# PV matmuls in two halves, the last output piece on other engines, and WoB's second half in five loads instead of eight

## The chip, the cores and the metric

One core of one Trainium2 chip. The metric is the device time of one execution in microseconds; the kernel before takes 473.68 us (median of 3, 473.41 to 474.09). The parts of the change discussed here are worth tenths of a microsecond, less than the scatter of single executions. So most of the argument rests on profiles: from one profile to another the length of a stage after the start-up repeats to 0.03 us or better, unless PE (TensorE) loses time in a single *hole* (treated below), and that is fine enough to see each part.

## The reference

Two attention blocks on the same 2048 x 1024 input, 32 heads of 32, mixed by a gate.

```python
def _A_ref(x, wqkv, wo):            # linear attention
    ...
    kv = jnp.einsum("bhsd,bhse->bhde", pk, v); z = ...
    o = num / den
    return ... @ wo
def _B_ref(x, wqkv, wo):            # sliding window: 8 keys, 2 apart
    kg = k[:, :, idx_c, :]; vg = v[:, :, idx_c, :]
    attn = softmax(where(mask, einsum("bhsd,bhswd->bhsw", q, kg) * scale, -1e9))
    o = jnp.einsum("bhsw,bhswd->bhsd", attn, vg)
    return ... @ wo
g = sigmoid((x * gate_w).sum(-1, keepdims=True))
return g * a + (1 - g) * b
```

## The kernel before

The part that matters is the attention stage of block B. For each of eight chunks of four heads, 64 projection *steps* make q and k; each step is four matmuls of 64x64 weights on 512 columns. In the profile of this kernel the four of the stage's first step start 3 to 4 ns apart and are recorded as 0.40 us each, while the next steps come 0.216 us apart. Between steps, *events* are slipped in by step number: score batches (`scores`, up to 16 matmuls) and PV batches (`pv`, 32 small matmuls of 33 columns, or 16 for the last batch of a chunk).

```python
def pv(g):
    c, m0, n = BATCHES[g]
    pt, base, ns = PT[g % 2], BLOCKS[m0][0], n // 2
    o2 = po[:, :, 0:ns * 132].rearrange("p a (s i e) -> p a s i e", s=ns, i=4)
    for s_ in range(ns):
        for i in range(4):
            for dm in range(2):
                for par in range(2):
                    ...
                    nc.tensor.matmul(o2[64 * h:64 * h + w, par, s_, i, :], lhsT=pt[r, i, o:o + w],
                                     rhs=V[r, m, 4 * c + i, :], start=True, stop=True)
    ...   # VectorE: reciprocals and scaling out of po, then stores
# when (64 steps a chunk):
for g, (c, m, n) in enumerate(BATCHES):
    p_ = 64 * c + ((43, 55, 75, 86, 97) if c < KT - 1 else (43, 55, 75, 83, 92))[m // 4]
    events.append((p_, lambda g=g: scores(g)))
    events.append((p_ + (14 if c < KT - 1 or m < 8 else 12), lambda g=g: pv(g)))
```

WoB's second half is loaded near the stage's end by `load_wo(1, 0, 8)`: eight loads of 128x512 from SyncE. In the output stage each piece is scaled and stored by ScalarE and its queue; the last piece is 128x128.

```python
nc.scalar.activation(out=osb[:, 0:n], in_=st["ps"][:, 0:n], func=ACT.Copy, scale=omg[:, tb:tb + 1])
nc.scalar.dma_start(out=rows(out2, tb * P, (tb + 1) * P)[:, c0:c0 + n], in_=osb[:, 0:n])
```

The softmax here doesn't subtract the row's maximum and nothing guards it: scores larger than these inputs give would overflow.

## Time and profile before

| | before |
|---|---|
| time, median | 473.68 us |
| span of the profiled execution | 472.29 us |
| PE busy, share of the chain | 99%, 98% |
| attention stage (first q/k matmul to first output matmul) | 141.17 us |
| tail (end of the last matmul to end of span) | 2.96 us |

The page of the kernel before: the busy line, and the first line of the chain that ended last (its shares by engine).

```profile
PE 466.0 (99%) x5734; PEld 244.7 (52%) x5765; DVE 277.4 (59%) x601; ACT 169.1 (36%) x273; POOL 15.4 (3%) x30
PE 98%; DMA 1%; issue 0%; ACT 0%
```

PE never rests long enough to matter, so a change pays only where PE's own stream loses time, or after it has ended.

The timeline of PE and of its weight loads (PEld) around one PV batch; columns are start, duration (from the first start to the last end), engine, line, operation, tiles, shapes and count.

```profile
248.53 0.81 PE L388 MATMUL q_ps<-xT,WkB 64*64 64x512 bf16 x10
249.15 0.42 PE L467 MATMUL po<-V,PT 64*56 64x33 bf16 x32
249.38 0.85 PE L388 MATMUL q_ps<-xT,WkB 64*64 64x512 bf16 x12
...
248.94 0.53 PEld L467 LDWEIGHTS <-PT 64*56 64x56 bf16 x32
249.38 0.38 PEld L388 LDWEIGHTS <-WkB 64*64 64x64 bf16 x12
```

The first weight load of the PV batch starts at 248.94, 0.21 us before its matmul at 249.15: the load runs one projection step (0.216 us) ahead. After the batch the first projection weights are loaded at 249.38, just when their matmul starts: the lead is gone. The batch's 0.23 us (249.15 to 249.38) is what 32 matmuls take when four start every 28.5 ns, as the first ones do in the single records, and the loss shows in the next step, which in the single records starts 237 ns later instead of 216.

The ends of the attention stage, in the same view.

```profile
217.40 0.84 PE L388 MATMUL q_ps<-xT,WkB 64*64 64x512 bf16 x12
...
358.57 1.90 PE L585 MATMUL d_ps<-WoA,pqT 128*128 128x512 bf16 x7
```

The end of the program: the timeline from the last matmuls.

```profile
468.83 0.50 PE L585 MATMUL e_ps<-WoB,OBT 128*128 128x128 bf16 x6
469.37 0.37 ACT L590 ACTIVATE osb<-e_ps,omg 128x128 bf16<-128x128 f32 x1 [0.47 <-PE e_ps L585]
469.76 0.34 ACTq L592 DMA_DIRECT2D out_dram<-osb  x1
```

SyncE's waits and drains at the last line of the program (a wait is for a semaphore; the first of the last five here ends 0.022 us after the last store has landed), from the view of that line (operation, count, minimum/median/maximum in ns, first and last start).

```profile
L639 SPq EVENT_SEMAPHORE  x7: 17/28/16728, 454.5 to 472.2; - x7
L639 SPq DRAIN  x3: 7/7/7, 471.5 to 471.8; - x3
```

PE ends at 469.33, ScalarE scales, its queue issues at 469.76. SyncE's first final wait lasts 16.7 us; the first drain comes at 471.5.

SyncE's DMA issues around the end of the attention stage.

```profile
347.34 6.52 SPq L517 DMA_DIRECT2D WoB<-in_B_wo_dram  x10
353.97 5.36 SPq L490 DMA_DIRECT2D obd<-Ob  x10
361.57 1.20 SPq L495 DMA_TRANSPOSE OBT<-obd  x1
```

### The profile page before, as it was taken

The page shows a single profiled execution, that of the slowest core. Times are in us where ns is not written, and L with a number is a line of the kernel's source. Part 1 is how long each engine was busy: PE and PEld are TensorE (multiplying, and loading weights), DVE is VectorE, ACT ScalarE, POOL GpSimd, SP SyncE. Part 2 cuts the span into 40 slices and gives each one's busy share as a digit, 9 for nine tenths or more (in the row PEclk, how much of TensorE's full clock was granted, in tenths as well). Part 3 has the DMA queues.
Part 4 walks back from the last instruction along what each step waited for, and adds up shares of the span by engine and source line. Part 5 has one row for each costly group of instructions (what it writes and reads, how often), then busy time and mean ns, then how long its engine had stood idle before and what let it go on. Part 6 is the DMA issues. An engine that isn't in the chain of part 4 may idle for free.

```text
span 472.3 us, 13144 instructions
## 1 busy us (share of the span) xinstructions
PE 466.0 (99%) x5734; PEld 244.7 (52%) x5765; DVE 277.4 (59%) x601; ACT 169.1 (36%) x273; POOL 15.4 (3%) x30
## 2 busy tenths in 40 slices
PE   8999999999999999999999999999999999999997
PEld 5444444445444444445666666666664444444444
DVE  0496689990329999999567676767560049800000
ACT  1343321102443333333555555555551134221122
POOL 3300000500000000000000000000000000000000
PEclk9999999999999999999999999999999999999999
DMA  8999970000634233527326526452563933211001
GB/s 212 212 242 374 348 239 0 0 1 0 203 123 125 95 141 129 156 96 247 107 54 108 105 53 95 100 95 51 92 158 79 196 97 78 71 53 46 34 33 46
DMA packets 98780, 55.40 MB, mean 117 GB/s; under 512 B 70178, under 2 KB 90658, under 8 KB 98722
## 3 DMA queue, kind: packets, MB, share of 16 engines
q1 hardware_dynamic: 93282, 49.84, 41.1%
q10 hardware_dynamic: 5440, 4.72, 3.0%
q8 instruction: 45, 0.74, 0.7%
q14 instruction: 13, 0.11, 0.1%
HBM read 26.10 MB, written 15.86 MB: 89 GB/s over the span
## 4 chain that ended last, share of the span: by engine, by line
PE 98%; DMA 1%; issue 0%; ACT 0%
PE q_ps L388 27%; PE d_ps L585 12%; PE pk_ps L169 12%; PE p_ps L295 12%; PE g_ps L220 12%; PE e_ps L585 11%; PE p_ps L331 9%; PE po L467 2%; PE s2b L445 2%; DMA xT<-in_A_x_dram 1%; PE kv_ps L240 0%; PE w_ps L283 0%; ACT osb L590 0%
## 5 line engine op out<-in xcount | busy, mean ns | idle before, releaser
L388 PE MATMUL q_ps<-xT,WqB 64*64 64x512 bf16 x1024 | 68.3, 377 | 0.0
L388 PE MATMUL q_ps<-xT,WkB 64*64 64x512 bf16 x1024 | 67.9, 377 | 0.0
L156 DVE TENSOR_SCALAR e<-e 128x512 f32<-128x512 f32 x64 | 27.0, 423 | 64.3 <-ACT e L155 64.3
L295 PE MATMUL p_ps<-WvB,xT 128*128 128x512 bf16 x250 | 57.3, 379 | 0.5 <-issue 0.3
L169 PE MATMUL pk_ps<-WkA,xT 128*128 128x512 bf16 x251 | 55.6, 381 | 0.9 <-DMA xT<-in_A_x_dram 0.6
L220 PE MATMUL g_ps<-pk,xrow 128*128 128x512 bf16 x251 | 55.2, 379 | 0.3
L450 ACT ACTIVATE PT<-s2b 128x928 bf16<-128x928 f32 (+4 forms) x40 | 34.2, 854 | 45.5 <-PE s2b L445 45.5
L452 DVE TENSOR_TENSOR PT<-PT,mask 128x928 bf16<-128x928 bf16 (+4 forms) x40 | 23.6, 590 | 38.2 <-ACT PT L450 38.2
L331 PE MATMUL p_ps<-WqA,xT 128*128 128x512 bf16 x187 | 43.1, 379 | 0.3
L585 PEld LDWEIGHTS <-pqT 128*128 128x128 bf16 x272 | 26.0, 98 | 29.8 <-issue 0.4
L585 PEld LDWEIGHTS <-OBT 128*128 128x128 bf16 x272 | 26.0, 98 | 29.3
L169 PEld LDWEIGHTS <-xT 128*128 128x128 bf16 x256 | 25.1, 98 | 31.2 <-DMA xT<-in_A_x_dram 0.9
L220 PEld LDWEIGHTS <-xrow 128*128 128x128 bf16 x256 | 25.0, 98 | 30.2
L295 PEld LDWEIGHTS <-xT 128*128 128x128 bf16 x256 | 24.6, 98 | 30.0 <-issue 0.9
L388 PEld LDWEIGHTS <-WkB 64*64 64x64 bf16 x1024 | 31.7, 107 | 15.4 <-issue 0.4
L388 PEld LDWEIGHTS <-WqB 64*64 64x64 bf16 x1024 | 31.4, 106 | 15.4 <-issue 0.7
L155 ACT ACTIVATE e<-pk_ps 128x512 f32<-128x512 f32 x32 | 18.9, 597 | 40.8 <-PE pk_ps L169 36.6
L300 ACT CAST tmp<-p_ps 128x512 bf16<-128x512 f32 x32 | 18.8, 590 | 37.9 <-PE p_ps L295 29.2
L585 PE MATMUL d_ps<-WoA,pqT 128*128 128x512 bf16 (+1 forms) x133 | 30.7, 369 | 0.2
L585 PE MATMUL d_ps<-WoB,OBT 128*128 128x512 bf16 (+1 forms) x134 | 30.7, 369 | 0.1
L331 PEld LDWEIGHTS <-xT 128*128 128x128 bf16 x192 | 18.8, 98 | 22.7
L585 PE MATMUL e_ps<-WoB,OBT 128*128 128x512 bf16 (+2 forms) x133 | 29.7, 363 | 0.2
(62 smaller groups left out, 484.6 us busy)
## 6 DMA issues: line engine op xcount, KB each, us to landing
vd<-tmp SPq DMA_DIRECT2D x16, 264.0 KB
xrow<-in_A_x_dram SPq DMA_DIRECT2D x4, 1024.0 KB
out_dram<-osb ACTq DMA_DIRECT2D x31, 128.0 KB
pqd<-tmp SPq DMA_DIRECT2D x12, 256.0 KB
WvA<-in_A_wqkv_dram SPq DMA_DIRECT2D x2, 1024.0 KB
WoA<-in_A_wo_dram SPq DMA_DIRECT2D x2, 1024.0 KB
WvB<-in_B_wqkv_dram SPq DMA_DIRECT2D x2, 1024.0 KB
WqA<-in_A_wqkv_dram SPq DMA_DIRECT2D x2, 1024.0 KB
```

The costliest lines, as they stand in the source:

```text
L155: nc.scalar.activation(out=e[:], in_=pj[:], func=ACT.Exp)
L156: nc.vector.tensor_scalar(out=e[:], in0=e[:], scalar1=1.0, scalar2=1e-6, op0=ALU.min, op1=ALU.add)
L169: nc.tensor.matmul(pj[:], lhsT=xT[:, kt, t * P:(t + 1) * P], rhs=WkA[half][:, kt, :], start=(kt == 0), stop=(kt == KT - 1))
L220: nc.tensor.matmul(pj[:], lhsT=xrow[:, t, kt * P:(kt + 1) * P], rhs=pk[:, t, half * 512:(half + 1) * 512], start=(t == 0), stop=(t == NB - 1))
L295: nc.tensor.matmul(st["pj"][:], lhsT=xT[:, kt, t * P:(t + 1) * P], rhs=WvB[half][:, kt, :], start=(kt == 0), stop=(kt == KT - 1))
L300: nc.scalar.copy(out=v[:, half * 16:(half + 1) * 16, 0:Dh], in_=st["pj"][:].rearrange("p (h e) -> p h e", h=16))
L331: nc.tensor.matmul(st["pj"][:], lhsT=xT[:, kt, t * P:(t + 1) * P], rhs=WqA[half][:, kt, :], start=(kt == 0), stop=(kt == KT - 1))
L388: nc.tensor.matmul(banks[o][64 * j:64 * j + 64, :], lhsT=lhsT(r, kt, j), rhs=rhs(r, kt), start=first and kt == 0, stop=kt == KT - 1, skip_ ...
L445: nc.tensor.matmul(s2b[64 * par:64 * par + 64, pair, :, o:o + w], lhsT=kts[c][r, par, k0:k0 + 64], rhs=qz[r, :, par, q0 % 512:q0 % 512 + w ...
L450: nc.scalar.activation(out=pt[:, :, 0:W_], in_=s2b[:].rearrange("p a b s -> p (a b) s")[:, :, 0:W_], func=ACT.Exp, scale=SCALE)
L452: nc.vector.tensor_tensor(out=pt[:, :, 0:W_], in0=pt[:, :, 0:W_], in1=mask[:, None, base:base + W_].broadcast_to([P, 4, W_]), op=ALU.mult)
L585: nc.tensor.matmul(st["ps"][:, 0:n], lhsT=lhsT, rhs=W[c0 // 512][:, c, c0 % 512:c0 % 512 + n], start=(side == 0 and c == 0), stop=(side == ...
```

## The change

The intent: split each PV batch so that the weight loads can get ahead again between its halves (before, their lead of 0.21 us is gone when the batch ends); use engines that are idle at the end for the last piece; free SyncE earlier.

```diff
-            def pv(g):
+            def pv(g, only):
-                for s_ in range(ns):
+                for s_ in only:
...
+                if only[-1] < ns - 1:
+                    return
...
-                events.append((p_ + (14 if c < KT - 1 or m < 8 else 12), lambda g=g: pv(g)))
+                at = p_ + (14 if c < KT - 1 or m < 8 else 12)
+                apart = 2 if c < KT - 1 or m < 8 else 0
+                for k in range(n // 2):
+                    events.append((at + apart * k, lambda g=g, k=k: pv(g, (k,))))
...
-            load_wo(1, 0, 8)
+            load_wo(1, 0, 4)
+            nc.sync.dma_start(out=WoB[1][:, 4:KT, :],
+                              in_=B_wo[4 * P:, 512:1024].rearrange("(k p) n -> p k n", p=P))
...
+                    if i == len(parts) - 1:
+                        nc.vector.tensor_scalar(out=osb[:, 0:n], in0=st["ps"][:, 0:n], scalar1=omg[:, tb:tb + 1],
+                                                scalar2=None, op0=ALU.mult)
+                        nc.sync.dma_start(out=dst, in_=osb[:, 0:n])
+                        return
```

More of the change, by code (lines that the diff above doesn't have):

```diff
@@ L589, in mm @@
                     osb = work3.tile([P, 512], BF16, name="osb", tag="e")
+                    dst = rows(out2, tb * P, (tb + 1) * P)[:, c0:c0 + n]
+                    if i == len(parts) - 1:
[3 more added lines that the diff above has]
+                        return
                     nc.scalar.activation(out=osb[:, 0:n], in_=st["ps"][:, 0:n], func=ACT.Copy,
                                          scale=omg[:, tb:tb + 1])
-                    nc.scalar.dma_start(out=rows(out2, tb * P, (tb + 1) * P)[:, c0:c0 + n], in_=osb[:, 0:n])
+                    nc.scalar.dma_start(out=dst, in_=osb[:, 0:n])
                 def side(k):
```

## The prediction

> **What bounds it now.** TensorE. The page's busy table has PE at 99% of the 472.3 us span, the chain of waits is 98% PE, the granted clock is 1.0, and the view of waits gives PE almost no idle time. Other engines have slack. Only bubbles in TensorE's own stream and the tail after it can pay.
>
> **PV batches.** In the attention stage (217.4 to 358.6 us) the timeline of single PE instructions shows a four-matmul projection step every 216 ns, score batches without loss, and a loss at each PV batch of 32 matmuls. Four PV matmuls start every 28.5 ns, so 32 should take 228 ns. From the batch's start to the next projection it takes 230 to 240, and the next step is 13 to 24 too long: 254 in the mean (31 batches). Near matmul 29 the weight load no longer runs ahead of its matmul[...]. Eight batches of 16 cost 118 to 120, plus 4 in the next step: 123. A 32-batch two steps after a score batch costs no more (252) than one after twelve (254)[...]. Two halves: 246 against 254, 8.5 ns saved. Three last batches are not split apart, so 30 are: **0.26 us**, all on the PE chain.
>
> The second half ends two steps (0.43 us) later, but nothing new should wait: reciprocals and scaling mostly stood behind the mask multiply on VectorE anyway, and the slack before the next PV, which reuses the same PSUM tile, is some 0.5 us.
>
> **Last output piece.** Before: the last matmul ends at 469.34, ScalarE scales from 469.37 to 469.73, its queue issues at 469.76, the data land at 471.23. VectorE's 128x128 read of PSUM takes 0.285 us in this trace (a broadcast multiply) against ScalarE's 0.368, so scaling saves 0.08 us[...]. But SyncE's final waits are a list: the last store's semaphore stands in the first of five, and after it four more took 62 ns each before the drain at 471.54. In the changed kernel as built the last store has the fifth wait's semaphore, so 0.25 us of waits are over beforehand. Net: **0.15 us**, between -0.1 and +0.3.
>
> **WoB.** Three load issues fewer, some 0.46 us each on SyncE (timeline, 349 to 354). The last attention stores and transposes issue 1 to 1.4 us earlier (first transpose: 361.6). PE waits for none of them: **0 us**.
>
> **Prediction.** 473.68 - 0.26 - 0.15 = 473.25 us; range 472.7 to 473.9, since medians scatter by 0.3. Faster by over 2%: 0.5%; within 2%: 99%; slower by over 2%: 0.5%.
>
> **Right or wrong.** The timeline should show PV batches of 16, two steps apart, each about 119 ns with the next step within 5 ns of 216; the attention stage 0.2 to 0.3 us shorter; no PE wait on VectorE; the first transpose at 360 to 361; the last scaling 0.3 us on VectorE, and the last SyncE wait followed at once by the drain.
>
> **What would make it wrong.** [...] a half with its own start-up cost; the next PV, or projections, waiting for delayed VectorE work; a SyncE store issuing or landing slower than ScalarE's.

In the PV part 254 and 123 ns a batch are read from the trace, and 30 x 8.5 ns make the 0.26 us. In the part on the last piece the step shows 0.08 and 0.25 us, and its net of 0.15 us stands as the estimate. The sum is: 473.68 - 0.26 - 0.15 = 473.25 us.

## The result

473.20 us (median of 6, 472.93 to 473.48) against 473.67 (median of 6) for the kernel before. The ratio is 0.9989, 95% interval 0.9977 to 1.0002. A ratio here is the mean time of one kernel's fast runs over that of the other's of the same rounds, so it is not quite the ratio of the medians quoted. The profiled executions are all at granted clock 1.0.

The page of the changed kernel, first line of the chain:

```profile
PE 98%; DMA 1%; DVE 0%; issue 0%; DVEq 0%
```

The timeline at the place of the batch shown above (PE, then its weight loads):

```profile
248.35 0.63 PE L388 MATMUL q_ps<-xT,WkB 64*64 64x512 bf16 x8
248.78 0.29 PE L467 MATMUL po<-V,PT 64*56 64x33 bf16 x15
248.90 0.38 PE L388 MATMUL q_ps<-xT,WkB 64*64 64x512 bf16 x1
248.90 0.18 PE L467 MATMUL po<-V,PT 64*56 64x33 bf16 x1
248.92 0.61 PE L388 MATMUL q_ps<-xT,WkB 64*64 64x512 bf16 x7
249.33 0.29 PE L467 MATMUL po<-V,PT 64*56 64x33 bf16 x15
...
248.87 0.11 PEld L388 LDWEIGHTS <-WkB 64*64 64x64 bf16 x1
```

Two batches of 16 (15 and one, because the last PV matmul and the first projection matmul start almost together), two steps apart. The projection weights are now loaded at 248.87, 0.03 us before their matmul: a small lead is left.

The ends of the stage:

```profile
217.09 1.27 PE L388 MATMUL q_ps<-xT,WkB 64*64 64x512 bf16 x20
...
358.12 1.90 PE L592 MATMUL d_ps<-WoA,pqT 128*128 128x512 bf16 x8
```

The stage takes 141.03 us, 0.14 less than before: about half of the predicted 0.26. The end of the program:

```profile
468.38 0.50 PE L592 MATMUL e_ps<-WoB,OBT 128*128 128x128 bf16 x6
468.98 0.35 DVE L599 TENSOR_SCALAR osb<-e_ps,omg 128x128 bf16<-128x128 f32 x1 [57.58 <-PE e_ps L592]
469.36 0.36 SPq L601 DMA_DIRECT2D out_dram<-osb  x1
```

and SyncE's waits and drains at the last line:

```profile
L652 SPq EVENT_SEMAPHORE  x7: 17/28/28, 469.8 to 471.6; - x7
L652 SPq DRAIN  x3: 7/7/7, 470.9 to 471.2; - x3
```

PE ends at 468.88 and the span at 471.66: the tail is 2.78 us, 0.18 less. From PE's end to the issue it takes 0.476 us, not 0.435: VectorE starts 0.097 us after PE's end, ScalarE had started 0.038 after it. What is shorter comes after the landing. The single records of SyncE's last five waits (end times, us) show how:

```
before: last store landed 471.227; waits end 471.249  471.314  471.376  471.439  471.501; drain 471.538
after:  last store landed 470.833; waits end 469.800  469.864  469.926  469.990  470.877; drain 470.914
```

Before, the first wait held the last store's semaphore, and four more waits of some 62 ns each followed the landing. After, four are over when the store lands.

SyncE's issues:

```profile
350.94 5.93 SPq L492 DMA_DIRECT2D obd<-Ob  x10
359.54 1.19 SPq L497 DMA_TRANSPOSE OBT<-obd  x1
```

Counted from the stage's start, the first transpose issues 1.7 us earlier (142.45 us in, not 144.17). No PE wait changed with it: the output stage, from its first matmul's start to the last one's end, takes 110.76 us in both.

What is left of the difference between the two profiles lies before the change's reach: the stretch up to the first q/k matmul is 0.30 us shorter. That is start-up scatter, treated below. So the stage seemed to owe some 0.1 us, and who had earned the tail was open.

### The profile page after: what moved, and what is told of

Same layout as the page of the kernel before. It is cut to its first block, busy times and chain, and to the rows that moved or that the text cites. A ratio compares the mean times of both kernels' runs of the same rounds, so it can differ in the third digit from the quotient of the medians.

```text
span 471.7 us, 13176 instructions
## 1 busy us (share of the span) xinstructions
PE 467.6 (99%) x5765; PEld 251.1 (53%) x5765; DVE 278.4 (59%) x602; ACT 168.7 (36%) x272; POOL 15.3 (3%) x30
## 4 chain that ended last, share of the span: by engine, by line
PE 98%; DMA 1%; DVE 0%; issue 0%; DVEq 0%
PE q_ps L388 27%; PE d_ps L592 12%; PE p_ps L295 12%; PE pk_ps L169 12%; PE g_ps L220 12%; PE e_ps L592 12%; PE p_ps L331 9%; PE po L467 2%; PE s2b L445 2%; DMA xT<-in_A_x_dram 1%; PE kv_ps L240 0%; PE w_ps L283 0%; DVE osb L599 0%; DVEq L599 0%
## 5 line engine op out<-in xcount | busy, mean ns | idle before, releaser
L388 PE MATMUL q_ps<-xT,WqB 64*64 64x512 bf16 x1024 | 69.7, 377 | 0.0
L388 PE MATMUL q_ps<-xT,WkB 64*64 64x512 bf16 x1024 | 69.0, 376 | 0.0
L388 PEld LDWEIGHTS <-WkB 64*64 64x64 bf16 x1024 | 34.0, 107 | 11.6 <-issue 0.4
L388 PEld LDWEIGHTS <-WqB 64*64 64x64 bf16 x1024 | 32.5, 107 | 11.1 <-issue 1.0
```

The source lines that it names most:

```text
L388: nc.tensor.matmul(banks[o][64 * j:64 * j + 64, :], lhsT=lhsT(r, kt, j), rhs=rhs(r, kt), start=first and kt == 0, stop=kt == KT - 1, skip_ ...
```

## The experiments

Ten runs followed: nine other kernels, and the changed one again. All were correct. The stage and the tail are read from single records of each profile: the first q/k matmul's start to the first output matmul's start, and the last matmul's modelled end to the span's end.

| run | stage us | tail us | median us (runs) |
|---|---|---|---|
| before | 141.17 | 2.96 | 473.67 (6) |
| the change | 141.03 | 2.78 | 473.20 (6) |
| e1_halves | 140.85 | 2.96 | 473.16 (6) |
| e2_tail | 141.20 | 3.02 | 473.79 (6) |
| e3_wob | 141.19 | 2.72 | 473.72 (6) |
| e4_halves_wob | 140.82 | 2.73 | 473.31 (6) |
| e5_wob6 | 141.38 | 2.84 | one run |
| e6_apart1 | 140.82 | 2.73 | one run |
| e7_quarters | 141.47 | 2.73 | 473.36 (6) |
| e8_pv_at_scores | 141.71 | 2.96 | one run |
| after_again | 140.82 | 2.78 | 473.15 (5) |
| e9_warm42 | 141.06 | 2.73 | 473.23 (5) |

The kernel before had 473.88, 473.80 and 473.65 in the three sets of rounds (e1 to e4; e5 to e8; the last two). Where there was one run, its state is unknown, and only its stage and tail are used.

### One part at a time

**e1_halves**: the PV part alone.

```diff
-            load_wo(1, 0, 4)
-            nc.sync.dma_start(out=WoB[1][:, 4:KT, :], ...)
+            load_wo(1, 0, 8)
...   # and the last piece again on ScalarE
```

> PV in halves alone; loads and tail as before. Theory[...]: about 12.5 ns saved in each of 30 split batches, so the attention stage falls from 141.17 to about 140.79 us, unless the single 0.2 us hole seen once in the changed kernel's stage comes with the halves, then 141.03; the tail from the last matmul's end to the span's end stays 2.96 us; time -0.3 us or so against before. Rival (the halves give nothing, the gain was all in the tail): stage 141.1 to 141.2.

Measured: stage 140.85, tail 2.96; ratio 0.9982 (0.9965 to 0.9999). The halves give 0.33 us of stage and nothing in the tail. The first rival, that the halves give nothing, is out. There was no such hole this time, so the halves do not need to bring one.

**e2_tail**: the last piece alone.

```diff
-                apart = 2 if c < KT - 1 or m < 8 else 0
+                apart = 0
...   # and load_wo(1, 0, 8)
```

> Last piece scaled on VectorE and stored from SyncE alone; eight loads as before. Rival to the prediction's account of the tail: the engine change itself costs about 0.04 us and gives nothing, because in this build the last store's semaphore is again in the first of the five final waits: tail 2.96 to 3.05 us. The prediction's account (the new store brings the gain of 0.15 to 0.2 us): tail 2.75 to 2.8 us. Stage 141.17.

Measured: tail 3.02 us, 0.06 *longer* than before; ratio 1.0001 (0.9981 to 1.0022). In its build the last store's semaphore is back in the first of the five waits. Its records give 0.311 us from the landing to the drain, the same as in the kernel before, and 0.476 us from PE's end to the issue, as in the full change. The first of its final waits is again a long one, 1.09 us, in the view of its last line:

```profile
L650 SPq EVENT_SEMAPHORE  x7: 17/28/1092, 469.9 to 472.0; - x7
```

**e3_wob**: five loads alone.

```diff
-            load_wo(1, 0, 8)
+            load_wo(1, 0, 4)
+            nc.sync.dma_start(out=WoB[1][:, 4:KT, :], ...)
```

> Five loads for the second half of WoB alone. The prediction gave this part 0. New theory: three fewer DMA issues move the last store from the semaphore in the first final wait to the one in the fifth, so four waits of 62 ns are over before it lands: tail 2.96 - 0.23 = 2.72 to 2.75 us, shorter than in the full change (2.78). Prediction as put: tail 2.96. Stage 141.17.

Measured: tail 2.72 us, 0.24 shorter, with the last piece still on ScalarE; ratio 0.9997 (0.9977 to 1.0017). No final wait is long now:

```profile
L646 SPq EVENT_SEMAPHORE  x7: 17/28/28, 467.5 to 473.8; - x7
```

So the part to which the prediction gave nothing earned the whole tail gain, and the part to which it gave 0.15 us cost 0.06. The builds show the link: here DMA issues take eight semaphores in rotation (in the trace of the kernel before the last eight stores, landing from 454.50 to 471.23 us, use each of the eight once, the last one number 2, counted from 0), and three issues fewer move the last store from number 2, which SyncE waits for first, to number 7, which it waits for last. The full change has it on number 7 in its trace. (This run's time, 475.65 us in the profiled execution, is a slow start; see below.)

**e4_halves_wob**: the change without the moved piece.

```diff
-                    if i == len(parts) - 1:
-                        nc.vector.tensor_scalar(...); nc.sync.dma_start(out=dst, in_=osb[:, 0:n]); return
```

> The change without its move of the last piece. If the tail gain belongs to the loads: tail 2.72 to 2.75 us and stage 140.8 (141.03 with the hole), so a span 0.04 us shorter than the full change's, which no timing will resolve; time 0.3 to 0.6 us under before. If the gain belongs to the move: tail 2.96.

Measured: stage 140.82, tail 2.73; ratio 0.9998 (0.9975 to 1.0020), with two of its six runs at 475.14 and 475.20 (see the slow start below). The tail is 0.05 us shorter than in the full change, as e2 and e3 say. No timing here resolves so little.

### Is it the place in the list of waits?

**e5_wob6**: six loads, everything else as before.

```diff
-            load_wo(1, 0, 8)
+            load_wo(1, 0, 5)
+            nc.sync.dma_start(out=WoB[1][:, 5:KT, :],
+                              in_=B_wo[5 * P:, 512:1024].rearrange("(k p) n -> p k n", p=P))
```

> The kernel before with six loads instead of eight for WoB's second half. In this build the last store's semaphore stands in the third of the five final waits. Theory (the tail gain is the place in the list of waits, 62 ns each): tail 2.96 - 2 x 0.062 = 2.83 us, halfway between eight loads (2.96) and five (2.72). Rival (fewer or larger loads shorten the tail in some other way, such as less queued work): 2.7 to 2.75 us, near that of five loads.

Measured: tail 2.84 us. Eight loads put the last store's semaphore in the first wait, six in the third, five in the fifth; the tails are 2.96, 2.84 and 2.72, and from the landing to the drain it takes 0.311, 0.186 and 0.080 us. The place in the list settles it; fewer loads as such do not. (The stage of this run, 141.38, contains a hole, though its PV is not split.)

### What the halves win, and where it ends

**e6_apart1**: e4 with the halves one step apart.

```diff
-                apart = 2 if c < KT - 1 or m < 8 else 0
+                apart = 1 if c < KT - 1 or m < 8 else 0
```

> Halves and five loads, the halves one step apart instead of two. If the lead of the weight loads is back after one step[...], the stage is 140.8 us as with two steps. If one step of 0.216 us is too short[...], the second halves cost more and the stage is 140.95 to 141.1.

Measured: stage 140.82. One step, 0.216 us, already gives the next half what two steps give it (140.82 in e4 too).

**e7_quarters**: e4 with PV in pieces of eight, one step apart.

```diff
-                for k in range(n // 2):
-                    events.append((at + apart * k, lambda g=g, k=k: pv(g, (k,))))
+                for k in range(n):
+                    events.append((at + (k if apart else 0),
+                                   lambda g=g, k=k: pv(g, (k // 2,), (2 * (k % 2), 2 * (k % 2) + 1))))
...   # and pv(g, only, quads) loops over quads in place of all four heads
```

> Halves and five loads, but PV in pieces of eight matmuls, one step apart. If the loss is the lead that a long run of short matmuls eats up, a quarter costs about its 57 ns and the stage falls by up to a further 12 ns in each of 30 batches, to 140.5 to 140.7 us. Rival (each piece has a start-up cost of its own, some 4 ns or more): stage 140.8 to 141.0. Time 0.6 us or so under before if the first holds.

Measured: stage 141.47, with one large hole after the last full PV batch, in the PE timeline:

```profile
350.68 0.83 PE L388 MATMUL q_ps<-WqA,xT 64*64 64x512 bf16 x10
351.68 0.41 PE L388 MATMUL q_ps<-WqA,xT 64*64 64x512 bf16 x4 [0.17 <-issue]
```

To leave holes out, compare the start of the last score batch, counted from the stage's start: 132.804 us before, 132.452 in e4, 132.533 in e7. The quarters lose 81 ns against the halves, 2.7 ns in each of 30 batches, two cuts more each. So the rival holds: a piece has a cost of its own, and halves are the better cut. The ratio, 0.9990 (0.9960 to 1.0021), does not tell them apart.

A sum that fits all three, an estimate from these numbers (its 6 and 22 ns are chosen so that it fits, so it tests nothing): four PV matmuls start every 28.5 ns, so 32 need 228; a batch of 32 cost 254 in all. Thirty pairs of halves saved 352 ns, so a pair costs about 254 - 352/30 = 242; four quarters cost 2.7 more, 245. Take 4 ns per piece (the excess in the step after the lone batches of 16 before): quarters 228 + 16 = 244, halves 228 + 8 plus 6 for the lead that two halves still lose, a whole batch 228 + 4 plus 22 for the lead that it loses.

**e8_pv_at_scores**: the kernel before, with the first PV batch of each chunk straight behind a score batch.

```diff
-                events.append((p_ + (14 if c < KT - 1 or m < 8 else 12), lambda g=g: pv(g)))
+            for g, (c, m, n) in enumerate(BATCHES):   # after all the score events
+                p_ = ...
+                events.append((p_ + (12 if m == 0 else 14 if c < KT - 1 or m < 8 else 12), lambda g=g: pv(g)))
```

> The kernel before with the first PV batch of each chunk moved straight behind a score batch, no projection step between them. [...] such a PV loses 15 to 40 ns more than at its old place: from the score batch to the next one 5035 to 5060 ns against 5019. Short-lead account ([...]score matmuls start every 12.7 ns and leave the lead whole): no more loss, 5015 to 5025 ns.

The PE timeline of e8 where the score batch now leads into the PV batch, and the next score batch:

```profile
247.63 0.38 PE L445 MATMUL s2b<-qz,kt 64*64 64x112 bf16 x16
247.83 0.42 PE L467 MATMUL po<-V,PT 64*64 64x33 bf16 x32
...
252.66 0.39 PE L445 MATMUL s2b<-qz,kt 64*64 64x112 bf16 x16
```

and the same two score batches in the kernel before:

```profile
245.68 0.38 PE L445 MATMUL s2b<-qz,kt 64*64 64x112 bf16 x16
...
250.70 0.39 PE L445 MATMUL s2b<-qz,kt 64*64 64x112 bf16 x16
```

Measured in single records: 5034 to 5036 ns in six of the eight chunks, where the kernel before has 5019 to 5020 (the first chunk has 5047 against 5031; the third, 5060, has a small hole). So 14 to 17 ns more are lost: at the lower edge of the expectation's first band, 5035 to 5060, or just under it, and outside the 5015 to 5025 of the short-lead account. What is measured is that the same PV batch costs more straight behind a score batch. The author's reading, that the two share one lead, was not shown: a cost of going from one kind of small matmul straight to another was not tested apart. In the records of the second chunk, the weight loads' lead of 27 ns first shortens about 160 ns into the PV batch here (to 24 and 20 ns), and about 200 ns into it before. Once the lead is gone, weight loads follow each other every 8 ns in these records; counting the matmul of each, that is one instruction every 4 ns.

### The hole

**after_again**: the changed kernel unaltered.

> The changed kernel once more. If the 0.2 us hole in its attention stage (between the sixteenth and seventeenth score batch) is an accident of one execution, such as a late fetch of PE's instructions, it is gone or elsewhere: stage 140.80 to 140.85 us without a hole. If it belongs to the change, it is at the same place and the stage is again 141.03. Tail 2.78 us either way. Median 473.2 to 473.4.

Measured: stage 140.82, tail 2.78; 473.15 us (5 runs), ratio 0.9989 (0.9976 to 1.0001). The chain of waits around the place of the hole, in the first profile of the changed kernel:

```profile
274.22 0.20 PE s2b L445 x14
274.43 0.91 PE q_ps L388 x15
275.33 0.27 PE po L467 x12
```

and in this one:

```profile
274.01 0.20 PE s2b L445 x14
274.21 0.84 PE q_ps L388 x12
275.06 0.10 PE po L467 x9
```

The hole is gone: in single records it is 2.915 us from this score batch to the next one, as in the kernel before, against 3.105 in the first profile. The whole stage gain of the change is therefore 0.35 us, and the first profile showed 0.14 only because PE lost 0.19 us there and some 0.04 in the next stretch.

Five of the twelve profiles have a hole of 0.18 to 0.57 us in the stage (the change, e5, e7, e8, e9), also without split PV. Their places are not random. In e5, e7 and e8 the hole begins between the same two of the stage's matmuls, numbers 3897 and 3898 counted from 0, in the middle of a step. In e9, whose warm-up has five matmuls more, it comes five earlier. In the change's first profile it comes 2304 earlier, which is 18 times 128. A matmul and its weight load are two instructions in the trace, so the places lie whole blocks of 256 instructions apart. The profile has two DMA queues of the kind "instruction". The larger moved 45 packets of 16 KiB, 0.74 MB in all; the change's profile records 11,537 PE instructions (5765 matmuls, 5765 weight loads, 7 others), about 256 for each packet.

The packets' landings fit as well. Count the PE instructions started (twice the weight loads) when a packet lands, less 256 for each packet before it. In the profile of the kernel before this stays between 162 and 340 for all 45 packets, and that is why this queue is taken to carry PE's instructions; nothing in the profile names its engine. For packet 38 (from 0) this is 362, 362, 356 and 354 in e7, e8, e9 and e5, which have holes of 0.57, 0.37, 0.24 and 0.18 us; 346 in e1, which lost 0.03 us there, and in e6, which lost nothing; and 342 or less in the other six. For packet 20, 18 earlier, it is 386 in the change's first profile and 378 or less in all others. So in these twelve profiles the holes go with packets that land late by this count, from 354 on at the one place and at 386 at the other. No run delayed a packet on purpose, so that the late landing causes the hole was not shown, and why some land late stays open.

### The slow start, and a candidate

Single runs took 475 us or more, up to 476.5: of the kernel before 2 of 11, 3 of 11 and 0 of 9 in the three sets, one or two of six in e2, e3, e4 and e7, the only one of e8, none of 11 of the change. They count as fast runs and widen the intervals above. The profiled executions of e3 and e8 were among them. The chain of waits at the first projection matmuls, in e3 and then in the kernel before:

```profile
5.72 4.83 PE pk_ps L169 x12
```

```profile
5.56 3.16 PE pk_ps L169 x12
```

In e3 the first ten of these matmuls start 402 to 427 ns apart and then 216; in the kernel before two do; in seven of the twelve profiles none does. The wide spacing is about half the pace; what sets it was not shown, and the clause of the e9 expectation that named a cause is cut. The last warm-up matmul starts at 4.63 us in e3, and PE then waits for data, idle 0.78 us. But this idle time alone does not decide: it was 0.83 us in e1 and e4 and 0.91 in e2, which have no slow start. The spacing changes where the trace's record of the granted clock begins: at 9.95 us in e3, 10.11 in e8, 6.41 in the kernel before, and 3.7 to 5.2 us, before the projections, in the seven profiles without a slow start. What sets that moment was not tested. The profile's printed granted clock reads 1.0 all the while, in e3 too (4 to 10 us): the trace has no clock record before 9.95 us there, and the view counts time without one as full clock.

**e9_warm42**: e4 with a longer warm-up.

```diff
-            warm_up(37)
+            warm_up(42)
```

> Halves and five loads, with 42 warm-up matmuls instead of 37, a candidate to beat both. Some executions lose up to 2 us because the first ten projection matmuls start 427 ns apart instead of 216; the first ones come after PE sat idle for 0.5 to 0.8 us. [...] filling it leaves 0 to 3 slow starts and no run above 475 us, median 472.9 to 473.3. If not, single runs of 475 or more remain.

Measured: 473.23 us (5 runs, none above 473.62), ratio 0.9991 (0.9977 to 1.0004); no slow start in its profile. But the kernel before had none either in its nine runs of this set, so this proves nothing about the warm-up, and e9 is not shown to beat the change.

## Why the prediction was right, and where it was not

The time was right: 473.25 predicted, 473.20 measured, 473.15 in the repeat. It tests little: the stated range, 472.7 to 473.9, also holds the kernel before (473.67), so a change worth nothing would have passed too. That the center came so close is partly luck, since one part was too small and another was credited to the wrong edit. The steps under it were right in part.

- *What bounds it.* Right: PE is 98% of the chain in both. Outside the attention stage and the tail, the stages from the second matmul group to the output matmuls take the same time to 2 ns in all profiles.
- *PV batches, 0.26 us.* What was measured held: behind a split batch the projection weights are again loaded 0.03 us before their matmul, two steps are enough (one is, too: stage 140.82 us in both), and nothing on VectorE made PE wait. Why the lead is lost and comes back was not shown. The size was too small: 0.35 us (e4 and the repeat), 11.8 ns a batch instead of 8.5. The mis-sized term is the half's cost, 121 ns in place of 123. In the first profile a hole hid 0.21 us of the gain.
- *"Last output piece ... net: 0.15 us".* The sum came near the tail's 0.18 us, but the step failed: it credited the moved piece with a semaphore's place in the list of waits that this piece did not change. The move alone lengthened the tail by 0.06 us (e2): VectorE's 0.351 us saved almost nothing against ScalarE's 0.368, where 0.285 had been taken from another operation, and from PE's end to the issue it is 0.04 us longer.
- *"WoB ... 0 us".* Wrong, and the other side of the same error: it is right that PE waits for none of these loads, but three issues fewer shift the rotation of DMA semaphores, and that is worth 0.24 us at the end (e3, with e5 halfway as the wait list says). The first transpose came 1.7 us earlier, not 1 to 1.4, and gained nothing, as predicted.

Stage 0.35 and tail 0.18 make 0.53 us; the medians differ by 0.47 and 0.50. Which version is best is not settled by times: profiles put e4's tail 0.05 us ahead of the full change.

## What to carry to other kernels

Here a run of 32 tiny matmuls ate up the lead of PE's weight loads from about 200 ns into the batch; it paid to cut it in two with one or two steps of 0.216 us between (0.35 us in 30 batches), but not finer, since quarters lost 81 ns against halves. The end of this program held up to four serial waits of some 62 ns after the last store had landed, and which semaphore that store got decided how many: look at the built wait list, and test each part of a change alone before crediting it, because a part that "does nothing" may shift it. When the gain sought is tenths of a microsecond, compare stage lengths in several profiles, since one accidental hole in one profile can hide half of it.
